# A three-layer kernel on one Trainium2 core: weights' sums of squares move from ScalarE to TensorE, the low bits of all weight pairs move to ScalarE, and four weight splits move forward

## The chip, the cores and the metric

The kernel runs on one core of a Trainium2 chip. TensorE (PE) multiplies matrices and writes its results to PSUM banks; VectorE (DVE), ScalarE (ACT) and GpSimd (POOL) work elementwise; SyncE (SP) issues most of the DMAs. Each engine runs its own instructions in the order in which they were written, and they meet at semaphores. The metric is the device time of one execution in microseconds; lower is better.

## The reference, cut to what matters

```python
q_s = softmax(q, axis=-1); k_s = softmax(k, axis=seq)         # 8 batches, 8 heads, 576 tokens, 64 wide
x   = q_s @ (k_s.T @ v)                                       # heads side by side: 8 x 576 x 512
u   = x + real(fft(fft(x, axis=1), axis=2))
un  = (u - mean(u)) / sqrt(var(u) + 1e-6)
x   = u + relu(un @ w_ch1) @ w_ch2                            # w_ch1 512 x 2048, w_ch2 2048 x 512
xk, xr = mu_k*x + (1-mu_k)*x_prev, mu_r*x + (1-mu_r)*x_prev   # x_prev: the token before
out = sigmoid(xr @ w_r) * (relu(xk @ w_k)**2 @ w_v)
```

The weights W1 (`w_ch1`), W2 (`w_ch2`), `w_k`, `w_v` and `w_r` arrive in double precision. W1 and W2 have 16 row blocks of 128 x 512 each.

## The kernel before, in words

Tokens are taken in nine blocks of 512. For each block `mm1(f)` makes 128 of the 2048 hidden features (12 products of 512 columns, in block 0 24 of 256 columns), and `mm2(f)` adds them into four accumulator banks; `mm2` runs two steps behind `mm1`. Every operand is split into a high and a low half-precision part, so one product is three.

Ahead of that stands a front part, in which nothing can be multiplied by the weights. For batch 0 `attention` makes the softmaxes and `U[0]`, `transform` does the two Fourier transforms as products with tables, `norm` normalizes, and `halves_part` writes `unh` and `unl` for `mm1`. `front_z` decodes W1 and W2 beside it, in 16 pairs of row blocks (pair k is `pairs[k]`; 0 to 7 are W1's, 8 to 15 W2's). A pair arrives as raw words, and becomes single precision in two steps of `assemble`. `low_parts(k)`: DVE shifts the high word into place (L168), and the three low bits are added, either by DVE itself (L170, `own`) or by ACT, which writes them beside the raw words (L172). `high_parts(k)`: DVE joins the rest (L174); after ACT's L172 it has to wait for that. In the kernel before, the even pairs are DVE's own and the odd ones take ACT. Then `squares` lets ACT square the pair and sum along the rows (L234, with a read of the accumulator behind it), and after eight pairs `scales` makes from the sum a power of two for the matrix. With it `split` writes one row block as two half-precision parts: the high one on ACT (L260), the low one on DVE (L261). The main loop starts when four blocks of W1 and two of W2 are split; the other 26 are split between its steps.

`beside_first` takes turns between the front part of batch 0 and steps of `front_z`, and in the main loop `side` does attention, transform and norm of the next batches. This is the order of the code only. The order on each engine is settled by a scheduler from its own estimates of time, so what comes of a change of the code is seen in the finished program. Small products of the front go to PSUM banks `side` and `acc`, while `h` has two banks in turn, for `mm1` and for the products that `warm` makes without use.

In `split` the step from ACT to DVE and on is:

```python
nc.scalar.activation(out=h, in_=st, func=AF.Copy, scale=s)
nc.vector.scalar_tensor_tensor(out=l, in0=st, scalar=s, in1=h, op0=ALU.mult, op1=ALU.subtract)
```

Of the kernel before, what the change touches and what calls it, by code (L numbers as in the profile page):

```python
# [8 lines left out]
F32 = mybir.dt.float32  # L9
F32R = mybir.dt.float32r  # L10
F16 = mybir.dt.float16
BF16 = mybir.dt.bfloat16
U32 = mybir.dt.uint32
U16 = mybir.dt.uint16
AF = mybir.ActivationFunctionType
ALU = mybir.AluOpType
AX = mybir.AxisListType
# [11 lines left out]
POOL_K = ()  # L29
BEHIND_X = {(1, 1): 6}  # L30
RATE = 0.4
OWN = 0
AHEAD_W = 6
FIRST = 1.0
HOLD = {(2, 0): "c"}
# [12 lines left out]
def net(ctx, tc, q, k, v, w1, w2, mu_k, mu_r, w_k, w_v, w_r, ce_d, se_d, cs_d, ss_d, alt_d, id_d, out):  # L48
    nc = tc.nc
# [13 lines left out]
    def bank(tag, bufs, shape=(128, 512)):  # L63
        return ps.tile(list(shape), F32, tag=tag, name=tag, bufs=bufs)
# [12 lines left out]
    mm = nc.tensor.matmul  # L77
# [14 lines left out]
    big = main.enter_context(tc.tile_pool(name="big", bufs=1, side="right"))  # L92
# [17 lines left out]
    wr = big.tile([128, len(order) + 1, 512], U32, name="wr", tag="w")  # L110
    wf = wr.bitcast(F16)
    onesr = big.tile([128, 128], F32R, name="onesr")
    ones = onesr.bitcast(F32)
    amax = big.tile([128, 2, 8], F32, name="amax")
    wsc = big.tile([128, 8], F32, name="wsc")

    ident = fc.tile([128, 128], F32, name="ident")
# [45 lines left out]
    def assemble(raw, x, part=None, own=False):  # L163

        hi, lo = raw[..., 1], raw[..., 0]
        join = nc.vector.scalar_tensor_tensor
        if part != 1:
            nc.vector.tensor_scalar(out=x, in0=hi, scalar1=3, scalar2=0x3FFFFFFF, op0=ALU.logical_shift_left, op1=ALU.bitwise_and)  # L168
            if own:
                join(out=x, in0=lo, scalar=29, in1=x, op0=ALU.logical_shift_right, op1=ALU.bitwise_or)  # L170
            else:
                nc.scalar.activation(out=raw.bitcast(U16)[..., 2], in_=lo, func=AF.Copy, scale=0.9975 * 2.0 ** -29, bias=-0.49)  # L172
        if part != 0:
            join(out=x, in0=hi, scalar=0xC0000000 if own else 0xC0000007, in1=x, op0=ALU.bitwise_and, op1=ALU.bitwise_or)  # L174
# [6 lines left out]
    pairs = [(w, c) for w in range(2) for c in range(0, 16, 2)]  # L181
    raws = {}
# [17 lines left out]
    def load_pair(k):  # L200

        if k >= len(pairs):
            return
        if k == 0:
            raws["places"] = word_places()
        w, c = pairs[k]
        raw = raws[k] = next(raws["places"]).rearrange("p (c n w) -> p c n w", c=2, w=2)
        for x in range(2):
            z = c + x
            if w == 0:  # L210
                src = w1.bitcast(U32)[128 * (z % 4):128 * (z % 4) + 128, 1024 * (z // 4):1024 * (z // 4) + 1024]
            else:
                src = w2.bitcast(U32)[128 * z:128 * z + 128, :]
            nc.sync.dma_start(out=raw[:, x].rearrange("p n w -> p (n w)"), in_=src)

    def words_at(w, c):
        a, b = place[w, c] + 1, place[w, c + 1] + 1
        return wr[:, a:b + 1:b - a]

    def low_parts(k):  # L220

        if k < len(pairs):
            assemble(raws[k], words_at(*pairs[k]), 0, k % 2 == OWN)

    def high_parts(k):
        if 0 <= k < len(pairs):
            assemble(raws.pop(k), words_at(*pairs[k]), 1, k % 2 == OWN)
            if k + 4 >= AHEAD_W:
                load_pair(k + 4)

    def squares(w, c):

        dump = wr[:, 0].bitcast(BF16).rearrange("p (c n) -> p c n", c=2)
        nc.scalar.activation(out=dump, in_=words_at(w, c).bitcast(F32), func=AF.Square, accum_out=amax[:, w, c // 2:c // 2 + 1])  # L234

    def scales(w):


        ts = nc.vector.tensor_scalar
        m = wsc[:, 3 * w:3 * w + 1]  # L240
        inv = wsc[:, 3 * w + 1:3 * w + 2]
        mi, ii = m.bitcast(U32), inv.bitcast(U32)
        nc.vector.tensor_reduce(out=m, in_=amax[:, w, :], axis=AX.X, op=ALU.add)
        pt = aside(False, 0)[:, 0:1]
        mm(out=pt, lhsT=one, rhs=m, start=True, stop=True)
        ts(out=inv, in0=pt, scalar1=2.0 ** -120, scalar2=None, op0=ALU.max)
        ts(out=mi, in0=ii, scalar1=1, scalar2=0x3F800000, op0=ALU.logical_shift_right, op1=ALU.bitwise_and)
        ts(out=ii, in0=mi, scalar1=0x7F800000, scalar2=None, op0=ALU.bitwise_xor)

        ts(out=inv, in0=inv, scalar1=(2.0 ** -55, 2.0 ** -51)[w], scalar2=None, op0=ALU.mult)  # L250
        ts(out=m, in0=m, scalar1=(2.0 ** 54, 2.0 ** 50)[w], scalar2=None, op0=ALU.mult)
        if w == 1:
            nc.vector.tensor_tensor(out=wsc[:, 6:7], in0=wsc[:, 0:1], in1=m, op=ALU.mult)

    def split(w, c):
        k = place[w, c]
        st = wr[:, k + 1].bitcast(F32)
        s = wsc[:, 3 * w + 1:3 * w + 2]
        h, l = wf[:, k, 0:512], wf[:, k, 512:1024]
        nc.scalar.activation(out=h, in_=st, func=AF.Copy, scale=s)  # L260
        nc.vector.scalar_tensor_tensor(out=l, in0=st, scalar=s, in1=h, op0=ALU.mult, op1=ALU.subtract)  # L261
# [182 lines left out]
    def warm(b, x, src):  # L444

        if b == 0:
            pt = bank("h", 2)
            if len(src.shape) > 2:
                src = src.rearrange(("p a b -> p (a b)", "p a b c -> p (a b c)")[len(src.shape) - 3])
            for _ in range(x):  # L450
                mm(out=pt[:, 0:128], lhsT=ones, rhs=src[:, 0:128], start=True, stop=True)
# [512 lines left out]
    def front_z():  # L964
        for k in range(len(pairs) + 2):
            if k < len(pairs):
                low_parts(k)
            high_parts(k - 1)
            if k >= 2:
                squares(*pairs[k - 2])  # L970
            yield 0
            if k - 2 in (7, 15):
                scales((k - 2) // 8)
                yield 0
        for c in range(4):
            split(0, c)
            yield 0
        for c in range(2):
            split(1, c)
            yield 0  # L980
        started[0] = True
        have[:] = 4, 2
        for g in range(1, NF // 4):
            for z in range(4):
                split(1, 4 * g - 2 + z)
                have[1] += 1
                yield 0
                split(0, 4 * g + z)
                yield 0
            have[0] += 4  # L990
        for c in (NF - 2, NF - 1):
            split(1, c)
            have[1] += 1
            yield 0
        front_left[0] -= 1
        stage.close()
        W["fx"] = front.enter_context(tc.tile_pool(name="fx", bufs=1))
# [11 lines left out]

    nc.scalar.preload_act_table_set("natural_log_exp_and_others")  # L1010
    sx, sy, sz = front_x(), front_y(), front_z()
    consts = load_constants()
    def latest(engines):
# [139 lines left out]
    words = big.tile([128, 31, 512], F32, tag="w", name="last")  # L1153
# [243 lines left out]
```

## Time and profile before

| | |
|---|---|
| median of 3 runs | 1457.01 us (1456.41 to 1457.19) |
| the profiled execution | 1457.53 us, of which the span from first to last instruction is 1455.8 us |
| PE busy | 1408.9 us, 97% |
| DVE busy | 992.0 us, 68% |
| ACT busy | 687.4 us, 47% |
| DMA | 89.47 MB, 61 GB/s over the span |

The span is what the instructions take on the core; the device time lies 1.7 us above it. Busy shares are averages over the whole span, in which the first hundred microseconds are unlike the rest, so stages have to be read apart.

### The profile page before, as it was taken

How to read it: one execution, taken by the hardware profiler on the slowest of the kernel's cores; microseconds unless marked ns; L12 is line 12 of the kernel's file. 1: busy time of each engine (PE TensorE's matmuls, PEld its weight loads, DVE VectorE, ACT ScalarE, POOL GpSimd, SP SyncE). 2: the span in 40 equal slices, each digit the busy share in tenths (PEclk: the TensorE clock that was granted, in tenths of full speed). 3: DMA queues.
4: the chain of work that ended last, by engine and by line, in shares of the span. 5: the costliest groups of instructions: out<-in, count | busy, mean ns of one | idle time of the engine just before them, and what ended most of it. 6: DMA issues, size and time to landing. Idle time of an engine off the chain costs nothing.

```text
span 1455.8 us, 21047 instructions
## 1 busy us (share of the span) xinstructions
PE 1408.9 (97%) x8519; PEld 883.1 (61%) x8519; DVE 992.0 (68%) x1804; ACT 687.4 (47%) x1233; POOL 26.3 (2%) x41
## 2 busy tenths in 40 slices
PE   4679999999999999999999999999999999999998
PEld 3568988886556556556555444445666666666665
DVE  8988686595683774753533476784999788875643
ACT  6776544453342433432322266573766555654422
POOL 1001000000000000000000000000000000000000
PEclk8699999999999999999999999999999999999999
DMA  9830013112011020110011032301011011100001
GB/s 376 297 124 2 18 42 108 54 58 72 17 52 64 27 71 35 52 46 1 0 59 38 15 115 74 116 23 58 30 59 59 22 38 59 52 8 30 29 17 42
DMA packets 38301, 89.47 MB, mean 61 GB/s; under 512 B 5147, under 2 KB 11580, under 8 KB 38204
## 3 DMA queue, kind: packets, MB, share of 16 engines
q1 hardware_dynamic: 37052, 85.30, 16.7%
q0 software_dynamic: 1152, 2.83, 0.6%
q8 instruction: 66, 1.08, 0.3%
q14 instruction: 31, 0.25, 0.1%
HBM read 69.25 MB, written 18.87 MB: 61 GB/s over the span
## 4 chain that ended last, share of the span: by engine, by line
PE 92%; DVE 4%; ACT 2%; issue 1%; DMA 0%; ACTq 0%; DVEq 0%
PE acc L1127 25%; PE h L1104 25%; PE acc L1230 13%; PE h L1165 11%; PE side L1218 6%; PE side L537 2%; PE side L517 2%; PE side L436 2%; PE side L381 1%; PE side L416 1%; DVE wr L174 1%; ACT wr L234 0%; DVE wr L261 0%; PE side L382 0%; ACT u L172 0%
## 5 line engine op out<-in xcount | busy, mean ns | idle before, releaser
L1104 PE MATMUL h<-unh,wr 128*128 128x512 f16 (+1 forms) x1408 | 380.0, 341 | 2.3 <-ACT wr L260 1.4
L1127 PE MATMUL acc<-hh,wr 128*128 128x512 f16 (+1 forms) x1408 | 368.6, 341 | 0.0
L1104 PEld LDWEIGHTS <-wr 128*128 128x128 f16 x2112 | 201.8, 98 | 165.5 <-issue 3.9
L1127 PEld LDWEIGHTS <-wr 128*128 128x128 f16 x2112 | 201.6, 98 | 159.9 <-issue 2.7
L1104 PE MATMUL h<-unl,wr 128*128 128x512 f16 (+1 forms) x704 | 239.3, 341 | 0.0
L1127 PE MATMUL acc<-hl,wr 128*128 128x512 f16 (+1 forms) x704 | 220.0, 341 | 0.0
L1230 PE MATMUL acc<-ring,last 128*128 128x512 f16 x864 | 201.2, 379 | 0.2 <-DVE last L1261 0.2
L1110 DVE SCALAR_TENSOR_TENSOR hl<-h,hh 128x512 f16<-128x512 f32 x144 | 99.1, 688 | 136.0 <-ACT hh L1109 135.2
L1109 ACT ACTIVATE hh<-h 128x512 f16<-128x512 f32 x144 | 85.7, 595 | 170.6 <-PE h L1104 170.1
L1230 PEld LDWEIGHTS <-last 128*128 128x128 f16 x864 | 84.0, 98 | 86.5 <-DVE last L1261 0.7
L1165 PEld LDWEIGHTS <-wkh 128*128 128x128 f16 x1008 | 98.5, 98 | 34.1
L1259 ACT ACTIVATE last<-last,pw 128x512 f32<-128x512 f32 x72 | 51.5, 717 | 106.9 <-DVE last L1258 106.3
L1218 PE MATMUL side<-ring,x 128*128 128x512 f16 x432 | 101.1, 379 | 0.0
L1180 DVE TENSOR_TENSOR last<-h,last 128x512 f32<-128x512 f32 x90 | 61.8, 687 | 49.9 <-PE h L1165 49.8
L1165 PE MATMUL h<-x,wkh 128*128 128x256 f16 x560 | 95.7, 273 | 0.0
L1165 PE MATMUL h<-x,wkl 128*128 128x256 f16 x280 | 76.3, 273 | 0.0
L1165 PE MATMUL h<-last,wkh 128*128 128x256 f16 x448 | 76.1, 273 | 0.0
L1218 PEld LDWEIGHTS <-x 128*128 128x128 f16 x432 | 42.3, 98 | 42.5
L1261 DVE TENSOR_TENSOR last<-last 128x512 f16<-128x512 f32 x72 | 49.5, 687 | 22.1 <-ACT last L1260 21.7
L1165 PE MATMUL h<-last,wkl 128*128 128x256 f16 x224 | 61.1, 273 | 0.0
L894 ACT ACTIVATE aa<-y,ms 128x512 f32<-128x512 f32 x72 | 48.0, 712 | 17.5 <-DVE x L902 12.2
L409 ACT ACTIVATE qT<-side 128x512 fp32r<-128x512 f32 (+3 forms) x44 | 37.0, 840 | 38.3 <-PE side L416 27.7
(358 smaller groups left out, 2087.1 us busy)
## 6 DMA issues: line engine op xcount, KB each, us to landing
vt<-in_v_dram SPq DMA_DIRECT2D x16, 650.0 KB, 5.4
kt<-in_k_dram SPq DMA_DIRECT2D x16, 576.0 KB, 3.9
qt<-in_q_dram SPq DMA_DIRECT2D x16, 576.0 KB, 3.8
out_dram<-oo SPq DMA_DIRECT2D x36, 256.0 KB, 2.0
y<-yT SPq DMA_DIRECT2D x8, 1026.0 KB, 5.3
u<-in_w_dram SPq DMA_DIRECT2D x16, 512.0 KB, 6.2
words<-in_w_dram SPq DMA_DIRECT2D x10, 512.0 KB, 9.9
raw<-in_w_k_dram SPq DMA_DIRECT2D x16, 256.0 KB, 3.6
```

The source lines that it names most:

```text
L409: nc.scalar.activation(out=dst(qT), in_=src, func=AF.Copy)
L894: nc.scalar.activation(out=a, in_=y[:, t, 0:n], func=AF.Copy, scale=mu[:, w, 1, t:t + 1])
L1104: mm(out=pt[:, o:o + m], lhsT=a, rhs=c[:, t, o:o + m], start=(t == z == 0), stop=(t == 3 and z == 2))
L1109: ma = nc.scalar.activation(out=hh[:, 0:n], in_=pt[:, 0:n], func=AF.Relu)
L1110: mv = nc.vector.scalar_tensor_tensor(out=hl[:, 0:n], in0=pt[:, 0:n], scalar=0.0, in1=hh[:, 0:n], op0=ALU.max, op1=ALU.subtract)
L1127: mm(out=acc[x][:, o:o + m], lhsT=a, rhs=c[:, o:o + m], start=(f == z == o == 0), stop=(f == NF - 1 and z == 2), skip_group_check=(i < 2))
L1165: mm(out=pt[:, 256 * x:256 * x + 256], lhsT=c[:, u, 128 * x:128 * x + 128], rhs=d[:, u], start=(fresh and x == u == z == 0), stop=(last an ...
L1180: nc.vector.tensor_tensor(out=out, in0=view(pt), in1=addend, op=ALU.add)
L1218: mm(out=pt, lhsT=a[:, v, u, c, o:o + 128], rhs=w[:, t, :], start=(t == y == 0), stop=(t == 3 and y == 2))
L1230: mm(out=acc[x], lhsT=a[:, 128 * x:128 * x + 128], rhs=c[:, f, :], start=(f == z == 0), stop=(f == 7 and z == 2))
L1259: nc.scalar.activation(out=o, in_=o, func=AF.Square, scale=W["pw"][:, 10 + g:11 + g])
L1261: nc.vector.tensor_tensor(out=l2, in0=o, in1=h2, op=ALU.subtract)
```

## The change

`squares` no longer uses ACT: it takes the upper 16 bits of the pair's words as bf16 and multiplies each 128 x 128 piece by itself on PE, eight products a pair, all of a matrix added into one quarter of an `h` bank (`gram`) that is held until `scales` has read it. `scales` multiplies that bank by the identity and sums along the rows, two DVE instructions of 128 columns in place of one of 8. `warm`'s products share one held bank. `OWN` is empty, so all 16 pairs take ACT's L172 (L171 in the changed kernel), and DVE's L170 is gone. The splits of W1's first four row blocks no longer stand behind the decode but in steps 10 to 13 of `front_z`, between the decode of pairs 9 to 13.

```diff
-OWN = 0
+OWN = ()
-    amax = big.tile([128, 2, 8], F32, name="amax")
     def low_parts(k):
         if k < len(pairs):
-            assemble(raws[k], words_at(*pairs[k]), 0, k % 2 == OWN)
+            assemble(raws[k], words_at(*pairs[k]), 0, k in OWN)
     def high_parts(k):
         if 0 <= k < len(pairs):
-            assemble(raws.pop(k), words_at(*pairs[k]), 1, k % 2 == OWN)
+            assemble(raws.pop(k), words_at(*pairs[k]), 1, k in OWN)
     def squares(w, c):
-        dump = wr[:, 0].bitcast(BF16).rearrange("p (c n) -> p c n", c=2)
-        nc.scalar.activation(out=dump, in_=words_at(w, c).bitcast(F32), func=AF.Square, accum_out=amax[:, w, c // 2:c // 2 + 1])
+        if "gram" not in raws:
+            raws["gram"] = bank("h", 2)
+        words = words_at(w, c).bitcast(BF16).rearrange("p c (n h) -> p c n h", h=2)[..., 1]
+        for x in range(2):
+            for g in range(0, 512, 128):
+                z = words[:, x, g:g + 128]
+                mm(out=raws["gram"][:, 128 * w:128 * w + 128], lhsT=z, rhs=z, start=(c + x + g == 0), stop=(c + x == 15 and g == 384))
     def scales(w):
-        nc.vector.tensor_reduce(out=m, in_=amax[:, w, :], axis=AX.X, op=ALU.add)
+        dg = wr[:, 4 * w, 0:128].bitcast(F32)
+        nc.vector.tensor_tensor(out=dg, in0=raws["gram"][:, 128 * w:128 * w + 128], in1=ident, op=ALU.mult)
+        nc.vector.tensor_reduce(out=m, in_=dg, axis=AX.X, op=ALU.add)
     def warm(b, x, src):
         if b == 0:
-            pt = bank("h", 2)
+            if "idle" not in raws:
+                raws["idle"] = bank("h", 2)
+            pt = raws["idle"]
     def front_z():
             if k >= 2:
                 squares(*pairs[k - 2])
+            if 0 <= k - 10 < 4:
+                split(0, k - 10)
             yield 0
             if k - 2 in (7, 15):
                 scales((k - 2) // 8)
                 yield 0
-        for c in range(4):
-            split(0, c)
-            yield 0
         for c in range(2):
             split(1, c)
             yield 0
```

Three places show how instructions now stand; lines of the changed kernel are one lower in `assemble` and six to eight higher behind `scales`. First ACT, in batch 0's attention. `qT` are transposed queries, `qt` and `kt` the exponentials of queries and keys, `kvbd` the copies of k'v, `words`, `u` and `raw` the places of raw pairs. Before:

```order
L370 ACTIVATE kt<-kt 128x1152
L409 ACTIVATE qT<-side_194 128x4x128
L409 ACTIVATE qT<-acc_204 128x4x128
L409 ACTIVATE qT<-acc_210 128x2x64
L363 ACTIVATE qt<-qt 128x1152
L172 ACTIVATE words<-words 128x1024
L391 ACTIVATE kvbd_98<-acc_175,rk 64x64 x4
L352 ACTIVATE m<-ident,wsc 128x128 x2
L234 ACTIVATE wr,amax<-wr 128x1024
L437 ACTIVATE u<-side_213 128x288
```

and of the change:

```order
L376 ACTIVATE kt<-kt 128x1152
L171 ACTIVATE words<-words 128x1024
L415 ACTIVATE qT<-side_193 128x4x128
L415 ACTIVATE qT<-acc_211 128x4x128
L415 ACTIVATE qT<-acc_217 128x2x64
L369 ACTIVATE qt<-qt 128x1152
L171 ACTIVATE words<-words 128x1024
L397 ACTIVATE kvbd_97<-acc_174,rk 64x64 x4
L358 ACTIVATE m<-ident,wsc 128x128 x2
L171 ACTIVATE u<-u 128x1024
L443 ACTIVATE u<-side_220 128x288
```

Pair 0's low bits now stand ahead of the query copies, and pair 2's stand ahead of the copies into `U[0]`, where before a pass of squares stood.

Second DVE, in the same stretch (pairs 1 to 3). Before:

```order
L170 SCALAR_TENSOR_TENSOR wr<-words,wr 128x1024
L168 TENSOR_SCALAR wr<-words 128x1024
L385 RECIPROCAL rk<-rk 128x2
L349 TENSOR_REDUCE wsc<-acc_243 128x2
L174 SCALAR_TENSOR_TENSOR wr<-words,wr 128x1024
L372 TENSOR_REDUCE st<-qt 128x18
L168 TENSOR_SCALAR wr<-u 128x2x512
L174 SCALAR_TENSOR_TENSOR wr<-words,wr 128x1024
L373 TENSOR_SCALAR st<-st 128x18
L170 SCALAR_TENSOR_TENSOR wr<-u,wr 128x2x512
L168 TENSOR_SCALAR wr<-u 128x2x512
L374 RECIPROCAL st<-st 128x18
```

and of the change:

```order
L173 SCALAR_TENSOR_TENSOR wr<-words,wr 128x1024
L391 RECIPROCAL rk<-rk 128x2
L355 TENSOR_REDUCE wsc<-acc_264 128x2
L378 TENSOR_REDUCE st<-qt 128x18
L167 TENSOR_SCALAR wr<-u 128x2x512
L173 SCALAR_TENSOR_TENSOR wr<-words,wr 128x1024
L379 TENSOR_SCALAR st<-st 128x18
L173 SCALAR_TENSOR_TENSOR wr<-u,wr 128x2x512
L380 RECIPROCAL st<-st 128x18
L167 TENSOR_SCALAR wr<-u 128x2x512
L382 TENSOR_TENSOR qt<-qt,st 128x1152
L173 SCALAR_TENSOR_TENSOR wr<-u,wr 128x2x512
```

Every L173 is now a join that needs ACT's L171 of its pair, and batch 0's own steps (L379 to L382) stand between such joins.

Third ACT, where the main loop begins. `unh` is the operand of `mm1`, `hh` the hidden features of one f, `wr` the splits. Before:

```order
L682 ACTIVATE unh<-d 128x2x256 x2
L260 ACTIVATE wr<-wr,wsc 128x512
L391 ACTIVATE kvbd_98<-side_756,rk 64x64 x4
L260 ACTIVATE wr<-wr,wsc 128x512
L437 ACTIVATE u<-side_818 128x288
L409 ACTIVATE qT<-side_792 128x4x128
L363 ACTIVATE qt<-qt 128x1152
L260 ACTIVATE wr<-wr,wsc 128x512
L437 ACTIVATE u<-side_815 128x288
L437 ACTIVATE u<-side_834 128x288
L260 ACTIVATE wr<-wr,wsc 128x512
L1109 ACTIVATE hh<-h 128x512
```

and of the change:

```order
L690 ACTIVATE unh<-d 128x2x256 x3
L369 ACTIVATE qt<-qt 128x1152
L1116 ACTIVATE hh<-h 128x512
L266 ACTIVATE wr<-wr,wsc 128x512
L397 ACTIVATE kvbd_97<-side_851,rk 64x64 x4
L1116 ACTIVATE hh<-h 128x512
L443 ACTIVATE u<-side_913 128x288
```

Between the last `unh` and the first `hh` stood five splits and a good part of batch 1's attention; now only an exponential of batch 1's queries stands there, and the first split behind it is W2's.

## Rows read from the trace of the kernel before

**Rows 1.** The page: span, busy time, granted clock in 40 slices.
```profile
span 1455.8 us, 21047 instructions
PE 1408.9 (97%) x8519; PEld 883.1 (61%) x8519; DVE 992.0 (68%) x1804; ACT 687.4 (47%) x1233; POOL 26.3 (2%) x41
...
PEclk8699999999999999999999999999999999999999
```

**Rows 2.** Busy time by stage (windows).
```profile
core 0: us, PE busy (x) PEld busy (x) DVE busy (x) ACT busy (x) POOL busy (x), PEclk, DMA share, GB/s
103.70:109.00 5.30, 3.10 (x17) 2.03 (x18) 4.07 (x7) 4.27 (x9) 0.00 (x0) 1.00 0.62 220
109.00:147.20 38.20, 36.62 (x312) 31.18 (x310) 32.74 (x56) 25.32 (x48) 4.52 (x2) 1.00 0.01 2
147.20:1455.80 1308.60, 1304.30 (x7864) 795.72 (x7862) 862.33 (x1581) 585.16 (x1056) 16.23 (x24) 1.00 0.14 46
```

**Rows 3.** Groups of DVE, 17.9 to 103.7 us: busy, mean ns, idle before.
```profile
L174 DVE SCALAR_TENSOR_TENSOR wr<-u,wr 128x1024 uint32<-128x1024 uint32 x8 | 9.7, 1214 | 0.9 <-ACT u L172 0.8
...
L174 DVE SCALAR_TENSOR_TENSOR wr<-words,wr 128x1024 uint32<-128x1024 uint32 x5 | 6.1, 1220 | 1.3 <-ACT words L172 1.3
...
L170 DVE SCALAR_TENSOR_TENSOR wr<-u,wr 128x1024 uint32<-128x1024 uint32 x4 | 4.9, 1216 | 0.0
...
L261 DVE SCALAR_TENSOR_TENSOR wr<-wr,wsc 128x512 f16<-128x512 f32 x2 | 1.5, 748 | 0.1
```

**Rows 4.** Groups of ACT, same stretch.
```profile
L234 ACT ACTIVATE wr<-wr 128x1024 bf16<-128x1024 f32 x16 | 17.1, 1070 | 1.5 <-DVE wr L174 1.4
L172 ACT ACTIVATE u<-u 128x1024 uint16<-128x1024 uint32 x4 | 10.0, 2496 | 0.3 <-DVE wr L168 0.3
...
L234 ACT ACTIVATION_READ_ACCUMULATOR wr<-wr 128x1 f32 x16 | 3.0, 190 | 0.0
```

**Rows 5.** Timeline at the decode's start: start us, us, instruction.
```profile
17.91 0.68 DVE L168 TENSOR_SCALAR wr<-words 128x1024 uint32<-128x1024 uint32 x1
...
18.12 1.11 ACT L409 ACTIVATE qT<-side 128x512 f32<-128x512 f32 x1 [4.84 <-PE side L416]
...
20.14 1.15 ACT L363 ACTIVATE qt<-qt 128x1152 f32<-128x1152 f32 x1
...
24.05 0.98 ACT L391 ACTIVATE kvbd<-acc,rk 64x64 f32<-64x64 f32 x4
...
25.06 0.69 ACT L352 ACTIVATE m<-ident,wsc 128x128 f32<-128x128 f32 x2
```

**Rows 6.** Timeline around pair 5: the store, ACT's next, DVE's join.
```profile
37.32 2.49 ACT L172 ACTIVATE words<-words 128x1024 uint16<-128x1024 uint32 x1
...
39.54 1.13 ACT L234 ACTIVATE wr<-wr 128x1024 bf16<-128x1024 f32 x1
39.85 1.23 DVE L174 SCALAR_TENSOR_TENSOR wr<-words,wr 128x1024 uint32<-128x1024 uint32 x1 [0.85 <-ACT words L172]
```

**Rows 7.** Timeline: four places that batch 0's front part passes.
```profile
45.15 1.04 ACT L391 ACTIVATE kvbd<-acc,rk 64x64 f32<-64x64 f32 x4 [1.27 <-DVE rk L385]
...
85.08 0.75 DVE L564 TENSOR_TENSOR u<-u,sd 128x574 f32<-128x574 f32 x1
...
102.16 0.28 DVE L619 TENSOR_TENSOR sq<-u 128x128 f32<-128x128 f32 x1
...
102.42 1.29 DVE L683 TENSOR_TENSOR unl<-d,unh 128x512 f16<-128x512 f32 x2
```

**Rows 8.** Timeline of PE, 36 to 108 us: products of attention.
```profile
36.29 2.10 PE L381 MATMUL acc<-vt,kt 128*128 128x130 f32 x8 [3.39 <-ACT kt L370]
...
98.19 1.06 PE L381 MATMUL side<-vt,kt 128*128 128x130 f32 x8
...
107.92 1.24 PE L436 MATMUL side<-qT,kvbd 128*128 128x288 f32 x4 [0.80 <-ACT qT L409]
```

**Rows 9.** The chain that ended last: 24 products of 256 columns.
```profile
141.90 2.62 PE h L1104 x24
```

## The prediction, made before the run

> **What bounds the kernel now.** I read the page first: PE is busy 1408.9 us of 1455.8, so what a change is worth elsewhere is only what it does to PE's idle time [rows 1]. The windows show where that is. From 147.2 us to the end PE idles 4.3 us in 1308.6, and from 109 to 147.2 only 1.6; before 109 it is starved, as in 103.7 to 109, with 3.10 busy of 5.30 [rows 2]. So the end is set by when PE can begin its dense run. It needs `unh`/`unl` of block 0, whose last part DVE finishes at 102.42 + 1.29 = 103.7 [rows 7], and the first splits. The groups of the stretch before say how DVE fares there: it waits little for ACT, 0.9 and 1.3 us ahead of 13 joins [rows 3]. DVE's queue is the front part's bound, with ACT close behind it early on.
>
> **What the change removes and adds, by sums.** DVE loses L170, eight of 1.22 us [rows 3]; the records overlap, so some 1.13 each: 9.0. ACT loses 16 squares with their reads, 17.1 + 3.0 = 20.1 us, and gets eight more stores of low bits of 2.50, 20.0 [rows 4]: its sum stays. DVE gets two more splits ahead of the halves (four of W1's instead of two; 0.75 less overlap, 1.35), and two diagonals of 128 columns with a sum each, which I price at 0.28 per instruction from the nearest row of 128 columns [rows 7], less two small sums: +0.8; nothing at the lowest, 1.4 at most. Four small steps of W2's scale (0.6) slip behind the halves. The 128 new products on PE have no row. Products of 256 columns take 2.62/24 = 0.109 us [rows 9]; half the columns, between 0.055 and 0.22 at half the clock, so 0.4 to 1.8 us a pair, in a stage where PE mostly waits. They delay others only where they stand ahead of a product that is ready; I found none in the new order that would be late by more than half a microsecond, so nothing in the sum, and +1 at its upper bound. `h`'s held bank has been read at about 106.1 in the reckoning below, ahead of the first `unl`, so `mm1(0)` does not wait for it. The DMAs are the same ones; pair k+4 loads after pair k's join, early by at least 8 us everywhere, hidden by the decode itself. If the sums decided, the halves would be finished by 9.0 - 1.35 - 0.8 + 0.6 = 7.4 us earlier.
>
> **The hand-offs.** But the order matters. A pair on ACT passes DVE (shift), ACT (store), DVE (join), and both engines go strictly down their queues. A store holds ACT 39.54 - 37.32 = 2.2 us, and its join starts 2.5 after the store did [rows 6]. Before, every second pair skipped ACT, and its L170 was work that filled DVE's time. Now all 16 take it. I walk the new queues, with durations from the rows.
>
> Pair 0's shift ends at 17.91 + 0.68 = 18.6 [rows 5], so its store runs from 18.6, and is ahead of the three query copies: these start at 20.8, not 18.12, and the exponential at 22.8, not 20.14 [rows 5]. Then pair 1's store 23.9 to 26.1, the copies to `kvbd` at 26.1 (before 24.05), two diagonals, and pair 2's store at 27.7. Its join can start at 30.2; DVE has had nothing to do since 27.6 (pair 1's join, from 26.4, and one small step) and waits 2.6. Behind that join stand pair 3's shift and a query multiplication, so pair 3's store starts at 32.2 and its join at 34.8, after 1.4 of waiting; behind that join stands pair 4's shift, so ACT in turn waits until 36.6. Pair 5's join waits 2.8. `kvbd`'s second half comes at 48.1 instead of 45.15 [rows 7]: +3.0. Going on in this way, the joins of pairs 0 to 15 wait 0.6, 0.5, 2.6, 1.4, 0.3, 2.8, 1.5, 0.3, 2.6, 1.3, 0.5, 1.5, 0.1, 0.4, 0 and 0.4: 16.8 us against 2.2 before. The transform's last addition to `u` (85.08 [rows 7]) comes at 91.8, +6.7, and the last `unl` ends at 110.6 instead of 103.7, +6.9. As a sum: 16.8 - 2.2 of waits, less the 7.4 above: +7.2. The two ways agree within 0.3.
>
> **A rule against a row.** The stores carry all this: 2.50 us each [rows 4]. The Trainium skill, page "ScalarE: Activation LUTs", section "What ACT_TABLE_LOAD costs", gives an activation with immediate scale and bias 186 ns + 0.833 ns per column, here an estimate of 1.04 us. At that price most of the joins' waits would be gone and the first rival's time would hold. The trace does not agree, with 2.50 in each such group, and the measurement decides.
>
> **From the halves to the end.** At 111.3 PE has done the 24 products of f=0 and two more. Before, by 109 it had done 22 of these (2.4 us), batch 1's k'v (two sets of 1.06 and their rests, 2.2 [rows 8]), three pairs of products into `U[1]` (1.24 for two of four, so 1.5 [rows 8]) and a transposition (0.4): 6.5 against 2.8, so 3.7 us of work are still to do. On the other hand W1's first splits no longer hold PE up. What is late next is `hh(0)`: on ACT an exponential of batch 1's queries is ahead of it, which waits for DVE's subtraction (115.0), which stands behind a step that needs batch 1's k'v (113.5 on PE). So `hh(0)` ends at 116.7, `hl(0)` at 118.2 and the first split of W2 at 118.9, while f=1's products are done by 115.9: PE waits 1.4 + 0.6 + 0.5 = 2.5. The same work that took from 109 to 147.2, 36.6 busy [rows 2], then ends at 111.3 + 3.7 + 2.5 + 36.6 = 154.1, against 147.2: +6.9. Behind it PE is dense in both, so nothing is given back. On the profiled execution's own 1457.5 that makes 1464.4; the median lies 0.5 below that execution, so **1463.9**.
>
> **Rivals.**
> 1. *The sums decide.* The hand-offs hide behind other work, the halves come 7.4 us earlier, and by the same steps the work of 147.2 ends at 139.8: 1449.6. For it: joins hardly wait now, DVE is the bound, and its work falls by 7.4. Against it: half the pairs make no hand-off now, and in the new queue an engine cannot pick other work. The point from which it decides is 9.6 us of waits at the joins in place of 16.8 (2.2 + 7.4): below it the front part shortens. Chance 0.18.
> 2. *Waits partly filled, by a faster PE.* The granted clock is 8 and 6 tenths in the first two slices of 36 us and 9 or more behind them [rows 1]; the two levels are 1.2 and 2.4 GHz, and the products of k'v take 2.10 us there and 1.06 later [rows 8]. 128 more products in those gaps may lift it. In the walk PE's products set a step at `U[0]`'s copies and in the transform's second stage, 1 to 2 us each, so the halves would come at +3.5: end at about 1460.4. The Trainium skill ("TensorE: Matmul & The Clock Gate", section "What's actually happening") says that the slow clock is the default and activity lifts it; the granted clock agrees, with 9 tenths or more from 73 us on, where PE is busy. For it: PE's gaps get shorter. Against it: eight products are under 2 us a pair, and the pairs are 4 to 7 us apart. Chance 0.16.
> 3. *Worse than the walk.* Thirty hand-offs at 0.05 to 0.1 us more each, the new products at their upper bound, and stage two at the half clock (+1.1 in the walk): +4, over 1467. Chance 0.06.
>
> **How the numbers follow.** The forecast has 0.60, with its own range 1460.5 to 1467: the walk with 3 us more (the products' upper bound, half the clock in stage two, slower hand-offs) or 3 less. A difference of 0.2% (2.9 us) is about the least that a measurement of this kernel can tell from no change. Slower by more than that, over 1459.9: the forecast, half of the second rival and the third, 0.60 + 0.08 + 0.06 = 0.74. Within: the other half of the second, and of the first the part in which the joins' waits end up near 9.6 us, 0.08 + 0.02 = 0.10. Faster: the rest of the first, 0.16. The range for 8 in 10 runs from 1453 to 1467.5: the forecast, the second rival and a quarter of the first; the rest of the first and the third lie outside.
>
> **What would show it.** Right: in the changed profile DVE's idle time before the joins (L173), put down to ACT L171, is 13 to 20 us up to the halves; `kvbd`'s second copies start near 48, the last `unl` ends between 109 and 112; PE's dense run begins there, with a wait for `hh(0)` or the first split of W2 near 116 to 119; from 155 on PE is as dense as now. Wrong: a last `unl` before 104 with joins that wait less than 9.6 us (rival 1); a granted clock at full before 60 us with copies into `U[0]` earlier than in the walk (rival 2); stores that take clearly less than 2.5; or a PE that idles between 120 and 155 for splits, which would put the loss in the main loop and not in the front part.

## The result, and the profile after

| | before | changed |
|---|---|---|
| median | 1456.71 us (1456.18 to 1457.19, 4 runs) | 1465.48 us (1465.1 to 1467.48, 4 runs) |
| ratio | | 1.0062, 95% interval 1.0046 to 1.0078 |
| the profiled execution, and its span | 1457.53, 1455.8 us | 1465.1, 1463.3 us |

The changed kernel is slower by some 0.6%, 8.8 us in the medians and 7.5 us in the profiled spans. The page of its profile: span, busy time and granted clock in 40 slices [before: rows 1].

```profile
span 1463.3 us, 21265 instructions
PE 1413.6 (97%) x8647; PEld 889.5 (61%) x8647; DVE 983.8 (67%) x1798; ACT 689.2 (47%) x1209; POOL 26.5 (2%) x41
...
PEclk8799999999999999999999999999999999999999
```

DVE has 8.2 us less to do in the whole, ACT's sum stays, and the core takes longer. The groups of DVE from 17.9 to 111 us say where (busy, mean ns of one, idle before and its cause), to be held against [rows 3]:

```profile
L173 DVE SCALAR_TENSOR_TENSOR wr<-u,wr 128x1024 uint32<-128x1024 uint32 x8 | 9.8, 1224 | 8.8 <-ACT u L171 8.8
L173 DVE SCALAR_TENSOR_TENSOR wr<-words,wr 128x1024 uint32<-128x1024 uint32 x5 | 6.1, 1226 | 5.2 <-ACT words L171 5.2
...
L173 DVE SCALAR_TENSOR_TENSOR wr<-raw,wr 128x1024 uint32<-128x1024 uint32 x3 | 3.7, 1224 | 2.8 <-ACT raw L171 2.8
...
L248 DVE TENSOR_TENSOR wr<-h,ident 128x128 f32<-128x128 f32 x2 | 0.6, 280 | 0.0
L249 DVE TENSOR_REDUCE wsc<-wr 128x1 f32<-128x128 f32 x2 | 0.6, 276 | 0.0
```

The joins wait 8.8 + 5.2 + 2.8 = 16.8 us for ACT's stores, where they waited 2.2. ACT's stores of the same stretch, and PE's new products:

```profile
L171 ACT ACTIVATE u<-u 128x1024 uint16<-128x1024 uint32 x8 | 19.9, 2493 | 1.2 <-DVE wr L167 1.1
L171 ACT ACTIVATE words<-words 128x1024 uint16<-128x1024 uint32 x5 | 12.4, 2482 | 6.4 <-DVE wr L167 6.4
...
L171 ACT ACTIVATE raw<-raw 128x1024 uint16<-128x1024 uint32 x3 | 7.5, 2495 | 3.4 <-DVE wr L167 3.3
...
L238 PE MATMUL h<-wr 128*128 128x128 bf16 x128 | 11.8, 247 | 12.1 <-DVE wr L173 12.1
```

Ahead of these stores ACT waits 10.8 us for DVE's shifts. Of these, 5.3 lie ahead of the very first store, where the decode begins and where ACT waited as long before (4.84, [rows 5]):

```profile
18.66 2.48 ACT L171 ACTIVATE words<-words 128x1024 uint16<-128x1024 uint32 x1 [5.34 <-DVE wr L167]
```

The other 5.5 us (with half the stores before, 3.3) stand against DVE's 16.8: the two engines pass a pair to and fro, and at times one stands still while the other works. The places in the timeline that answer to [rows 7], and the last part of `unl`:

```profile
47.94 1.05 ACT L397 ACTIVATE kvbd<-acc,rk 64x64 f32<-64x64 f32 x4 [3.36 <-DVE rk L391]
...
91.11 0.75 DVE L572 TENSOR_TENSOR u<-u,sd 128x574 f32<-128x574 f32 x1
...
110.00 0.68 DVE L691 TENSOR_TENSOR unl<-d,unh 128x512 f16<-128x512 f32 x1
```

PE starts the first product of the main loop at 106.28 us, before at 98.08. From there to the end the two kernels are alike, in products, busy time and idle time (9.1 and 9.2 us). The windows of the kernel before, and of the changed one (the second of these starts where the same work is left as before at 147.2 [rows 2]):

```profile
98.08:1455.80 1357.72, 1348.53 (x8227) 832.48 (x8224) 904.77 (x1658) 617.80 (x1116) 20.75 (x26) 1.00 0.14 46
```

```profile
106.28:1463.30 1357.02, 1347.93 (x8227) 833.33 (x8227) 902.06 (x1655) 616.35 (x1113) 20.84 (x26) 1.00 0.14 46
152.40:1463.30 1310.90, 1304.47 (x7861) 795.71 (x7858) 863.56 (x1587) 587.62 (x1062) 16.23 (x24) 1.00 0.14 46
```

So the difference can be read in two numbers for each kernel: when the first product starts (+8.2), and how long the rest takes (-0.7). One thing belongs to the first number: the product at 106.28 waits 0.9 us for the bank `gram`, which DVE's second diagonal (L248) has read only then.

```profile
106.28 0.39 PE L1111 MATMUL h<-unh,wr 128*128 128x256 f16 x2 [0.93 <-DVE wr L248]
106.87 0.27 PE L1111 MATMUL h<-unl,wr 128*128 128x256 f16 x1 [0.20 <-DVE unl L691]
```

That costs next to nothing, since the third product waits for the first part of `unl` in any case, up to 106.8.

### The profile page after: what moved, and what is told of

Its sections match the earlier page's. It is cut to its first block, busy times and chain, and to the rows that moved or that the text cites. A ratio compares the mean times of both kernels' runs of the same rounds, so it can differ in the third digit from the quotient of the medians.

```text
span 1463.3 us, 21265 instructions
## 1 busy us (share of the span) xinstructions
PE 1413.6 (97%) x8647; PEld 889.5 (61%) x8647; DVE 983.8 (67%) x1798; ACT 689.2 (47%) x1209; POOL 26.5 (2%) x41
## 3 DMA queue, kind: packets, MB, share of 16 engines
q1 hardware_dynamic: 37052, 85.30, 16.8%
## 4 chain that ended last, share of the span: by engine, by line
PE 90%; DVE 4%; ACT 3%; issue 1%; DMA 1%; SPq 0%; ACTq 0%; DVEq 0%
PE h L1111 25%; PE acc L1134 24%; PE acc L1237 13%; PE h L1172 11%; PE side L1225 6%; PE side L525 2%; PE side L545 2%; PE side L387 2%; PE side L442 2%; ACT u L171 1%; PE side L422 1%; ACT words L171 1%; DMA kt<-in_k_dram 1%; PE side L388 0%; DVE wr L267 0%
## 5 line engine op out<-in xcount | busy, mean ns | idle before, releaser
L1266 ACT ACTIVATE last<-last,pw 128x512 f32<-128x512 f32 x72 | 51.6, 717 | 106.9 <-DVE last L1265 106.3
L1172 PEld LDWEIGHTS <-wkl 128*128 128x128 f16 x504 | 49.3, 98 | 6.4
```

Source lines behind the costliest of these rows:

```text
L1172: mm(out=pt[:, 256 * x:256 * x + 256], lhsT=c[:, u, 128 * x:128 * x + 128], rhs=d[:, u], start=(fresh and x == u == z == 0), stop=(last an ...
L1266: nc.scalar.activation(out=o, in_=o, func=AF.Square, scale=W["pw"][:, 10 + g:11 + g])
```

## The experiments

**Theory:** the stores of low bits, 2.5 us each and each between two steps of DVE, cost the time. **Rival 1:** the 128 products, or the bank that they hold. **Rival 2:** the four splits that now stand ahead of the halves. A third one was not named before the runs, that ACT simply has too much to do; it is taken up behind split_behind.

All runs in one table, from their profiles: what the joins waited in the front part, when the main loop's first product started, what the rest of the span took, and the median of all runs with its ratio to the kernel before. The first three columns come from one execution each, which need not be the median one: that of split_behind was the slowest of its four (1471.75), that of splits_only the slowest of its eleven (1458.5).

| run | joins wait | first product | the rest | median, ratio (95%) |
|---|---|---|---|---|
| before | 2.2 | 98.1 | 1357.7 | 1456.7 |
| changed | 16.8 | 106.3 | 1357.0 | 1465.5, 1.0062 |
| even_own | 3.5 | 100.2 | 1357.1 | 1460.2, 1.0022 (1.0012 to 1.0031) |
| own_four | 7.8 | 101.5 | 1357.7 | 1461.6, 1.0034 (1.0021 to 1.0048) |
| half_each | 1.1 | 100.3 | 1356.8 | 1459.7, 1.0017 (1.0007 to 1.0026) |
| half_store2 | 4.0 | 93.3 | 1357.4 | 1453.2, 0.9976 (0.9965 to 0.9986) |
| no_store | 0.1 | 90.0 | 1356.5 | 1448.2, 0.9937 (0.9923 to 0.995) |
| far_join | 0.3 | 105.8 | 1363.2 | 1473.2, 1.0111 (1.0097 to 1.0125) |
| all_act_alone | 19.7 | 107.1 | 1358.5 | 1468.0, 1.0076 (1.0062 to 1.0089) |
| split_behind | 18.9 | 106.8 | 1362.4 | 1470.1, 1.0087 (1.0072 to 1.0103) |
| gram_only | 3.5 | 98.7 | 1360.3 | 1461.1, 1.0032 (1.002 to 1.0045) |
| splits_only | 2.2 | 99.1 | 1357.6 | 1456.75, 0.9998 (0.9989 to 1.0007) |
| cheap_own | 6.1 | 100.2 | 1358.4 | 1461.3, 1.003 (1.0019 to 1.004) |

**even_own.** The changed kernel, with

```diff
-OWN = ()
+OWN = (0, 2, 4, 6, 8, 10, 12, 14)
```

> The changed kernel, but the even pairs' low bits are DVE's own again (eight L169 of some 1.2 us come back); the products on PE and the moved splits stay. Theory (the hand-offs cost it): the joins behind ACT's stores wait 2 to 4 us in all in place of 16.8, DVE's sum before the last unl is 1.6 us above that of the kernel before, so the last unl ends at 104 to 107 and the time is 1456 to 1460. Rival 1 (the 128 products, or the bank that they hold, cost it) and rival 2 (the splits that now stand ahead of the halves cost it): both stay, so the time stays at 1463 to 1466.

The joins wait 3.5, the last `unl` ends at 104.7, and 5.3 us of the loss are gone. The rivals' claim that nothing changes falls. What is left against the kernel before is 3.3 us, a little more than expected; gram_only looks for it.

**own_four.** The same with `OWN = (2, 5, 8, 11)`.

> The changed kernel with four pairs DVE's own (2, 5, 8 and 11, those whose joins waited longest or stood ahead of a step of batch 0) and twelve on ACT. Theory (hand-offs): the waits lie between the 16.8 of no own pair and the 3.5 of eight: 6 to 11 us, time 1458 to 1463. If the waits only move to other pairs, they stay near 14 to 17 and the time at 1464 to 1469. If four own pairs are enough, waits below 4 and 1453 to 1457, which beats both kernels.

Waits and start lie between none and eight own pairs: 16.8, 7.8 and 3.5 us of waits, first product at 106.3, 101.5 and 100.2. Going from four own pairs to eight moves the first product by only 1.3 us; each own pair also costs DVE a step of 1.2.

**far_join.** The joins forced one pair later:

```diff
-            high_parts(k - 1)
+            high_parts(k - 2)
...
+            with tc.issue_after(shifts[min(k + 2, 15)].ins):
+                assemble(raws.pop(k), words_at(*pairs[k]), 1, k in OWN)
...
```

The products and the moved splits follow the joins, so they too come one step later.

> The changed kernel, but each join stands one pair later on DVE, behind the shift of the pair after the next (an order that is forced), so that ACT has about two steps of the decode for its store. The same instructions, no work more or less. Theory (hand-offs): the joins wait 6 us or less in place of 16.8; the last unl ends 7 to 13 us earlier than in the changed kernel (98 to 104) and the time is 1449 to 1458. Rivals 1 and 2 (products or splits): no change, 1463 to 1467. If the raw pairs' places now come free too late, a wait for DMA takes the place: 1459 to 1463, with DVE's shifts put down to loads.

This went against the forecast by 15 us. The joins wait 0.3 us, and the first product still starts at 105.8. DVE's waits in the front part, by what was waited for:

```profile
DVE rk L393 <- PE acc L391: 7.2, 1, 7.2
DVE wsc L358 <- PE acc L356: 3.0, 1, 3.0
DVE yl L538 <- ACT yh L535: 2.3, 1, 2.3
DVE wr L169 <- DMA u<-in_w_dram: 2.0, 2, 1.3
DVE wr L270 <- ACT wr L269: 1.4, 1, 1.4
```

DVE has the same 73 us of work, and idles 19.0 of 91.9 us in place of 19.5 of 92.8. It now waits 7.2 us for batch 0's k'v, which waits for the exponential of the keys on ACT. That starts at 38.97 us, in the changed kernel at 41.07, behind five stores in either; in the kernel before it starts at 35.06, behind two stores and three passes of squares. The lines of far_join, the changed kernel and the one before:

```profile
38.97 1.15 ACT L379 ACTIVATE kt<-kt 128x1152 f32<-128x1152 f32 x1
```

```profile
41.07 1.14 ACT L376 ACTIVATE kt<-kt 128x1152 f32<-128x1152 f32 x1
```

```profile
35.06 1.18 ACT L370 ACTIVATE kt<-kt 128x1152 f32<-128x1152 f32 x1
```

The stores still stand in ACT's queue ahead of batch 0's steps, and in the forced order DVE has no other work then. So it isn't the joins' wait as such: a wait that is only moved comes back elsewhere. (The main loop behind it is worse as well, 1363.2; that the forced order is to blame for this was not tested.)

**half_store2.** ACT stores the low bits of only one of the pair's two row blocks:

```diff
-nc.scalar.activation(out=raw.bitcast(U16)[..., 2], in_=lo, func=AF.Copy, scale=0.9975 * 2.0 ** -29, bias=-0.49)
+y = raw[:, 0:1] if len(raw.shape) == 4 else raw
+nc.scalar.activation(out=y.bitcast(U16)[..., 2], in_=y[..., 0], func=AF.Copy, scale=0.9975 * 2.0 ** -29, bias=-0.49)
```

> The changed kernel with ACT's store of low bits cut to one row block of the two of a pair, 512 of 1024 columns (the lowest three bits of the other block are left out, and hold what the raw word has there). From 0.81 us for 256 columns and 2.49 for 1024 it should take some 1.37. Theory (hand-offs): 3 to 9 us of waits at the joins in place of 16.8, first product of the main loop at 96 to 101 in place of 106.3, time 1452 to 1459. Rivals 1 and 2 (products or splits): at most 1 to 2 us less than the changed kernel, 1463 to 1466.

**no_store.** The same with no store at all for W1 and W2.

> The changed kernel without ACT's store for W1 and W2 (the lowest three bits of all their entries are left out): neither ACT nor DVE makes them, and no join waits for ACT. It is the end of the row 2.5, 1.4 and 0 us. Theory (hand-offs): DVE's sum alone is left, so the halves come 16.8 us earlier than in the changed kernel or up to where batch 0's own chain over PE and ACT holds them: first product at 89 to 95, time 1446 to 1453. Rivals 1 and 2: DVE does as much as in the changed kernel, and ACT was not the limit: 1461 to 1466.

Both times are as expected; no_store gives the joins' 16.8 us back nearly whole, and half_store2 starts its first product earlier than the 96 to 101 forecast. The first group of stores of half_store2, then the front part of no_store (span, PE, PEld, DVE, ACT, POOL busy; clock; DMA) beside that of the changed kernel:

```profile
L172 ACT ACTIVATE u<-u 128x512 uint16<-128x512 uint32 x8 | 10.8, 1355 | 4.7 <-DVE wr L167 3.6 <-issue 1.1
```

```profile
17.90:94.60 76.70, 60.43 (x440) 52.77 (x439) 73.23 (x136) 34.26 (x76) 4.71 (x8) 0.89 0.72 274
```

```profile
17.90:110.70 92.80, 63.49 (x435) 54.64 (x434) 73.33 (x132) 69.00 (x91) 4.85 (x8) 0.82 0.62 227
```

The stretch, up to the last `unl`, shrinks by 16.1 us while PE (with its 128 products) and DVE (with its moved splits) have the same instructions to do. DVE is busy as long as in the changed kernel (73.2 and 73.3 us); PE is 3 us less busy, at a higher granted clock (0.89 in place of 0.82). With a store of 2.49, 1.36 and 0 us the first product starts at 106.3, 93.3 and 90.0. Only the store differs (and the order, which the scheduler adapts to it), so both rivals fall for the changed kernel: with products and splits in place it is 8.1 us ahead of the kernel before once the store is gone.

**half_each.** The version of this that leaves nothing out: of each pair ACT stores one row block's low bits and DVE makes the other's.

```diff
+nc.scalar.activation(out=raw[:, 0].bitcast(U16)[..., 2], in_=raw[:, 0, :, 0], func=AF.Copy, scale=0.9975 * 2.0 ** -29, bias=-0.49)
+nc.vector.scalar_tensor_tensor(out=x[:, 1], in0=raw[:, 1, :, 0], scalar=29, in1=x[:, 1], ...)
...
```

> The changed kernel, but of each pair ACT makes the low bits of one row block and DVE those of the other, and the join is two instructions of 512 columns (nothing is left out). Each hand-off is of some 1.4 us in place of 2.5, and DVE has 0.65 us of the same pair's work to do meanwhile; DVE does some 10.5 us more of low bits than in the changed kernel and 1 to 2 us more for the joins' halves. Theory (hand-offs): waits below 4 us, first product at 99 to 103, time 1456 to 1461. If a hand-off costs the same however short the store is, waits stay over 10 and the time goes over 1466.

As expected: waits of 1.1 us, but DVE pays for it with its own work: 1459.7, 5.8 us less than the changed kernel and 2.8 more than the one before.

**all_act_alone.** The kernel before with `OWN = 2`, so no pair is DVE's own, and nothing else of the change.

> The kernel before, with one part of the change alone: all 16 pairs' low bits on ACT; the squares stay on ACT too, and the splits stay behind the decode. Theory (hand-offs): the joins wait at least as long as in the changed kernel, and longer where a pass of squares (1.07 us and a read) stands ahead of a store: 17 to 26 us in all, last unl at 110 to 117, time 1463 to 1472. Rivals 1 and 2 (products or splits cost it, and neither is here): DVE only loses 9 us, 1448 to 1457.

1468.0, +11.2: this part alone makes the loss, and with the squares still on ACT it makes more of it than the whole change.

**split_behind.** The changed kernel with the splits where they were:

```diff
-            if 0 <= k - 10 < 4:
-                split(0, k - 10)
...
+        for c in range(4):
+            split(0, c)
+            yield 0
```

(In this run the second diagonal's scratch lies on a row block of W1 that is not split yet, so that block's values are not the weights; the instructions are the same.)

> The changed kernel, but the four splits of W1 stand behind the decode again; all 16 pairs still take ACT. Theory (hand-offs): the joins still wait 14 to 18 us, DVE has two splits less ahead of the halves (1.35), but PE waits for splits at the loop's start again as in the kernel before; 1462 to 1466. Rival 2 (the splits ahead of the halves cost it): 1456 to 1460.

The waits are 18.9, a little above what was expected, and the time is 4 us above it: 1470.1, 4.6 above the changed kernel, by the rest (1362.4). The moved splits help here; rival 2 has the wrong sign. But the reason given does not show: of the 5.4 us that the rest is longer, 4.5 are busy time of PE (1352.4 us in place of 1347.9), with a granted clock of 0.93 up to 130 us where the changed kernel has 1.00, and only 0.9 is idle time.

```profile
106.83:1469.20 1362.37, 1352.43 (x8227) 834.53 (x8226) 905.44 (x1658) 618.72 (x1116) 21.11 (x26) 1.00 0.13 46
```

Every run that gave time back by shortening or dropping stores also left ACT less to do, so ACT's load as such is a rival. Two runs speak against it: split_behind is all_act_alone with the squares on PE. The front parts of all_act_alone and of split_behind:

```profile
17.90:112.80 94.90, 56.08 (x304) 47.60 (x302) 72.39 (x132) 84.76 (x122) 4.97 (x8) 0.80 0.61 225
```

```profile
17.90:112.10 94.20, 62.36 (x412) 52.71 (x411) 72.19 (x129) 68.98 (x90) 4.84 (x8) 0.81 0.59 223
```

With 15.8 us of squares taken off ACT the front part is 0.7 us shorter and the first product starts 0.3 earlier. Halving the stores takes about as much off ACT (17.5 us, half_store2 against the changed kernel) and lets the first product start 13.0 earlier.

**gram_only** and **splits_only.** The kernel before with one of the two other parts (the products come with their bank and their diagonals):

> The kernel before with the products alone: squares on PE, but the even pairs' low bits are DVE's own and the four splits stand behind the decode (the second diagonal's scratch is moved to a free place). It parts the 3.4 us that the run with even pairs on DVE still lies above the kernel before. If the splits ahead of the halves are these (1.35 of DVE's time, with the four small steps), 1455.5 to 1458. If the products and the diagonals are, 1459 to 1462. Joins wait 2 to 4 us in either case.

> The kernel before with the moved splits alone (the dump of the squares goes to other free places). With products alone at 1461.1 and both at 1460.2 it closes the square. If the splits ahead of the halves cost DVE 1.5 to 2 us there and spare PE as much behind them, 1456 to 1458.5. If the products cost nothing and the splits are what lies between 1456.8 and 1460.2, 1459 to 1462. If they spare PE more than they cost, 1453 to 1456, which would beat both kernels.

The splits alone change nothing that can be measured (0.9998). The products alone cost 4.5 us in the medians, 3.2 in the profiled spans, and not where expected: the first product of the loop starts 0.6 later, but the rest takes 2.6 more. The windows of gram_only, there and from the first product to the end, and one of the kernel before:

```profile
98.69:104.00 5.31, 4.76 (x36) 3.54 (x36) 5.31 (x16) 2.81 (x5) 0.00 (x0) 1.00 0.20 48
104.00:108.00 4.00, 1.72 (x7) 1.05 (x8) 3.85 (x6) 2.07 (x6) 0.00 (x0) 0.77 0.61 252
108.00:112.00 4.00, 4.00 (x29) 3.37 (x28) 3.17 (x5) 3.94 (x6) 0.00 (x0) 0.80 0.37 86
98.69:1459.00 1360.31, 1350.12 (x8225) 833.23 (x8225) 905.74 (x1657) 617.73 (x1116) 20.13 (x26) 1.00 0.13 46
```

```profile
104.00:108.00 4.00, 2.10 (x13) 1.33 (x13) 3.62 (x4) 3.15 (x8) 0.00 (x0) 1.00 0.52 168
```

PE waits for the splits (2.0 us for one of them, up to 105.9), and behind that gap its granted clock drops to the lower level (0.50 from 107 to 109 us) and is back at 1.00 by 110. Of the 2.6 us, 1.6 are busy time (1350.1 in place of 1348.5) and 1.0 is idle time. The idle time does not lie at the loop's start, where PE idles no longer than before in all (4.3 us up to 130 us, before 4.7), but between 300 and 350 us (1.3 us; there it is a wait for DVE's L417). That the gap makes the clock fall was not tested. With the splits moved too (even_own) the longest wait for a split is 0.9 us, and the clock stays at 1.00. Beside all_act_alone the two parts together save 2.5 us (1468.0 to 1465.5), beside own pairs they cost 3.3 (1456.8 to 1460.2): what a part is worth depends on which engine is late.

**store_forms.** ACT's store in four forms in one kernel.

> A price list, with output that is not the reference's: ACT's store of 1024 columns in four forms in one kernel. Pairs 0, 1, 14, 15 as they are (32-bit integers read at every second place, 16-bit integers written at every fourth); pairs 2 to 5 read integers that lie side by side; pairs 6 to 9 write side by side; pairs 10 to 13 read floats at every second place. The pass of squares that reads 1024 floats side by side and writes 16-bit values side by side took 1.07. If the place of what is read costs it, pairs 2 to 5 take about 1.1 and the others 2.5; if the place of what is written, pairs 6 to 9 do; if the conversion from integers, pairs 10 to 13; if two of these, none falls all the way.

ACT's instructions of that line: the count, then ns of the shortest, middle and longest.

```profile
L178 ACT ACTIVATE u<-u x4: 2497/2518/2547, 71.0 to 92.2; 128x1024 uint16<-128x1024 f32 x2, 128x1024 uint16<-128x1024 uint32 x2
...
L178 ACT ACTIVATE u<-wr x2: 2461/2494/2526, 27.8 to 32.2; 128x1024 uint16<-128x1024 uint32 x2
L178 ACT ACTIVATE wr<-u x2: 1100/1114/1127, 49.3 to 53.8; 128x1024 uint16<-128x1024 uint32 x2
```

Reading side by side (`u<-wr`) or floats changes nothing. Writing side by side (`wr<-u`) takes 1.11 in place of 2.50 (all four of these pairs: 1.10 to 1.17): the place of what is written makes the price.

**cheap_own.** A version that might beat both, built on the kernel before:

```diff
-join(out=x, in0=lo, scalar=29, in1=x, op0=ALU.logical_shift_right, op1=ALU.bitwise_or)
+half = raw.bitcast(U16)
+nc.vector.tensor_scalar(out=half[..., 2], in0=half[..., 1], scalar1=13, scalar2=None, op0=ALU.logical_shift_right)
...
-join(out=x, in0=hi, scalar=0xC0000000 if own else 0xC0000007, in1=x, op0=ALU.bitwise_and, op1=ALU.bitwise_or)
+join(out=x, in0=hi, scalar=0xC0000007, in1=x, op0=ALU.bitwise_and, op1=ALU.bitwise_or)
```

> The kernel before, and nothing of the change: squares on ACT, even pairs' low bits DVE's own, splits behind the decode. Only the form of DVE's own step is another: the upper 16 bits of the low word, shifted by 13, go as 16-bit integers to where ACT's store puts them (beside the raw high word), so the step takes one tensor and not two, and needs no ACT; nothing is left out. If a one-tensor step on 1024 columns costs what the shift does (0.68 in place of 1.22), DVE's sum ahead of the halves falls by 8 x 0.54 = 4.3 us without a hand-off: first product at 93 to 96, time 1451.5 to 1455, faster than both kernels. If DVE too pays for writing 16 bits at every fourth place, as ACT does, the step takes 1.2 us or more and the time is 1456 to 1460.

The dear case: the step takes 1.32 us, more than the 1.22 that it replaces. The time is 1461.3, and so 1.3 us above what was expected of this case: eight steps at 0.1 more are 0.8 us, but the joins now wait 6.1 us in place of 2.2. Why they do was not looked into.

```profile
L171 DVE TENSOR_SCALAR u<-u 128x1024 uint16<-128x1024 uint16 x4 | 5.3, 1318 | 0.0
```

No version here that leaves nothing out beats the kernel before.

## Why the prediction was right, step by step

- **The sums (-7.4 us).** DVE is busy 80.1 us up to the last `unl` before, and 73.3 in the changed kernel: 6.8 less. The kernel before, in that stretch:

```profile
17.90:103.70 85.80, 58.34 (x304) 48.78 (x302) 80.08 (x141) 67.32 (x114) 4.71 (x8) 0.78 0.68 252
```

  no_store agrees. Its joins wait 0.1 us, 2.1 less than before, and its last `unl` ends at 94.5, 9.2 earlier: that leaves 7.1 for the sums.

```profile
93.86 0.68 DVE L692 TENSOR_TENSOR unl<-d,unh 128x512 f16<-128x512 f32 x1
```

  (ACT is 35 us less busy there too, so this is not the sums alone.) A diagonal's instruction costs 0.28, as taken from the nearest row; a pair's products 11.8 / 16 = 0.74 us, within 0.4 to 1.8.
- **The hand-offs (16.8 us).** The sum of the waits came out at 16.8, and not by luck: join by join they lie within 0.3 us of the forecast, but for pairs 11 (2.2, forecast 1.5) and 15 (1.0, forecast 0.4). `kvbd`'s second half started at 47.94 (48.1 forecast), the last addition to `u` at 91.1 (91.8), and the last `unl` ended at 110.7 (110.6). The walk of the two queues with durations from the rows carried all of this; a balance of the sums would have given the wrong sign. But far_join shows that the waits are where the cost is read and not all that it is. The stores cost the time, by their length; how much of it by DVE's wait at the joins and how much by standing ahead of batch 0's steps in ACT's queue, no run parts.
- **The rule against the row.** The Trainium skill ("ScalarE: Activation LUTs", section "What ACT_TABLE_LOAD costs") made the store 1.04 us, an estimate. Where the store writes side by side it takes 1.10 to 1.17, 6 to 13% above that; where it writes at every fourth place the row's 2.50 holds, and with it the loss.
- **From the halves on, two sizes were off and nearly cancel, which is luck.** The start of the main loop was mis-sized: batch 1's k'v ran among f=0's products, at 109.6 to 112.0, so the subtraction that ACT's exponential waits for ended at 113.5 and not at 115.0, `hh(0)` at 115.2 and not 116.7, and PE waited 1.4 for a split of W2 in place of 2.5 in all:

```profile
112.14 1.35 DVE L368 TENSOR_TENSOR qt<-qt,st 128x1152 f32<-128x1152 f32 x1
...
113.53 1.16 ACT L369 ACTIVATE qt<-qt 128x1152 f32<-128x1152 f32 x1 [3.71 <-DVE qt L368]
...
114.60 0.58 ACT L1116 ACTIVATE hh<-h 128x512 f16<-128x512 f32 x1
...
115.84 1.05 PE L1134 MATMUL acc<-hh,wr 128*128 128x256 f16 x8 [1.41 <-ACT wr L266]
```

  The amount of PE's work that was left at 147.2 before is left at 152.4 now: +5.2, where +6.9 was forecast. "Behind it PE is dense in both" was wrong: from there to the end the changed kernel takes 1310.9 us and the one before 1308.6, 2.3 more. Near 337 us PE waits 2.2 us where the kernel before has no gap:

```profile
336.96 0.59 PE L1111 MATMUL h<-unh,wr 128*128 128x512 f16 x2 [0.32 <-ACT unh L690]
338.23 0.39 PE L525 MATMUL side<-seh,eh 128*128 128x256 f32 x1 [0.68 <-DVE yl L535]
340.39 0.38 PE L1111 MATMUL h<-unl,wr 128*128 128x512 f16 x1 [1.19 <-DVE unl L691]
```

  From 300 to 350 us PE idles 2.1 to 2.2 us in nearly every run that has the products or the moved splits or both (gram_only 1.3, in another wait; far_join 3.1), and not at all in the three that have neither (before, all_act_alone, cheap_own). So it comes with these two parts; by which step was not settled.

  The two make the span 7.5 us longer in place of 6.9. The rest of the 1.6 us between forecast (1463.9) and median (1465.5) is not the kernel's: the forecast put the median 0.5 below the profiled execution, as in the kernel before, and in the changed kernel it lies 0.4 above it. (In the kernel before four splits, not five, stood between the last `unh` and the first `hh`.)
- **The rivals.** The sums did not decide: 16.8 us of waits against the turning point of 9.6. PE's granted clock rose a little, to 0.74 from 17.9 to 60 us (0.65 before), not to the full level. The second copies into `U[0]` start at 50.4, 2.0 later than before, and the last `unl` is where the walk had it, so the second rival did not apply either.
- **What the text put at nothing.** The products were priced at nothing in the sum. no_store bears this out for the front part, and so do split_behind and all_act_alone, where the one with the products is not the later. That PE "mostly waits" there was too much said: it is busy 58.3 of 85.8 us. The held bank was forecast to be read before `mm1(0)` needs it; it was read at 106.2 and held the first product up by 0.9 us, without harm. In the kernel before the products cost 4.5 us (gram_only), which the profile finds in a later first product (0.6), the lower clock at the loop's start (1.6) and more idle time behind it (1.0), and not in their own time; the other 1.3 us are the distance of the two profiled executions from their medians.

## What to carry to other kernels

When work moves from one engine to another, count the hand-offs and walk both queues: a step that sits between two steps of one other engine costs its latency wherever neither queue holds other ready work (here 16.8 of the 40 us of stores), and two engines that are each under 80% busy can still hold each other up for 17 us. Price the step by a row with its own layout, since the same store took 1.1 or 2.5 us by where it writes. Test it by making the suspected step shorter rather than by moving the wait: the first gave the time back, the second only renamed it.

## What the chip showed that was not expected

- ACT's store of 1024 16-bit values takes 2.50 us at every fourth place and 1.11 side by side; whether it reads integers at every second place, integers side by side or floats changes nothing (store_forms). 512 values at every fourth place take 1.36 (half_store2).
- DVE shows the like in cheap_own: a one-tensor step of 1024 values takes 0.69 us from 32 bits to 32 bits side by side, and 1.32 from 16 bits to 16 bits at every fourth place. Whether width or place makes this was not parted.
- PE's clock can fall to the lower level inside the main loop's start: to 130 us the mean granted clock is 0.95 in gram_only, 0.93 in split_behind, far_join and all_act_alone, and 1.00 in the others. In gram_only PE had waited 2.0 us for one split before it fell; in the kernel before, PE's longest wait there is 1.2 us, and it did not fall. The products from the first of the loop to the end then took 1350.1 us of PE's time in place of 1348.5.
